# Decay rows by broadcast transfer, a shorter value product, and weight tails doubled by engines in a recurrent mixer with FFT and MLP

## The chip, the cores and the metric

One Trainium2 chip (trn2), one of its cores. The metric is the device time of one execution in microseconds. Three runs of the kernel before gave 452.97 to 453.72, median 453.53. A further execution was recorded by the hardware profiler.

## The reference

Three blocks follow one another on 4 batches, 768 positions, 8 heads of 40 (320 channels):

```python
for t in range(S):                       # 1: gated recurrent attention
    m_new  = np.maximum(f_gate[:, :, t] + m, i_gate[:, :, t])
    f_stab = np.exp(f_gate[:, :, t] + m - m_new)
    i_stab = np.exp(i_gate[:, :, t] - m_new)
    C = f_stab * C + i_stab * einsum(v, k);  n = f_stab * n + i_stab * k
    y[:, :, t] = sigmoid(o_gate) * (C q) / max(|n q|, 1)
gate = sigmoid(causal 5-tap convolution of x)      # 2: gated value
x    = (gate * (x @ w_val)) @ w_out
u  = x + real(fft(fft(x, axis=1), axis=2))          # 3: FFT mixing
un = layernorm(u)
out = u + relu(un @ w_ch1) @ w_ch2                  # 320 -> 1280 -> 320
```

All weights come as float64 bit patterns (two 32-bit words) and are turned into float32 on the chip.

## The kernel before, in words

**How it is written.** The functions in `mixer_kernel` only record instructions in units (`_Plan.add`). `_Plan.emit` (line 288) then issues the units in the order of the table `ORDER`, found beforehand; the table `CELL` gives every tile its slot of SBUF or bank of PSUM, and `FILLS` says where matmuls on a tile of ones stand that compute nothing. Each engine works through its own instructions in order. All instructions issued there have line 305 in the profile, so groups are told apart by tile names. Banks of PSUM are all called `bank`. Transfers are issued by SP, in order too.

**Attention.** It goes in chunks of 128 positions (`c` 0 to 5 for each batch `b`), each made of two halves of 64. `a_fb` puts the decay factors of 64 positions on all partitions (`fb`): in the first four chunks of batch 0 with 16 small float32 matmuls from `f0`, from then on with one 128x512 matmul of a 0/1 table `sel` and the rows `gsp`, which hold a high and a low part of the factors (`prologue_spread` writes both parts to a DRAM scratch `scr`, `gate_rows` loads them for a batch). `a_pre` runs a scan over `fb` on DVE, which gives the decay matrix `d`, and scales values and keys (`kvo`) on POOL. `a_pv` issues, on TensorE, the state product (`cc,e`), the scores of the next chunk (`qk`, in `s_mm`), in batches 1 to 3 the state update (`kvo`, in `u_mm`) and last `kvo,d`, which adds to the same PSUM columns from other rows of the array. Between `cc,e` and `kvo,d` TensorE must have finished: in batches 1 to 3 a `nop` on SP's queue (line 309) waits for the last matmul of the state product and releases the next group; in batch 0 and in the last chunk of each batch a `drain` on TensorE does so. `a_fin` divides by max(|nq|, 1).

**Gated value** (twice a batch, 384 positions each): `p_conv` (four taps of five on DVE, 128x384), `p_val` (for each of three blocks `j` of channels 8 matmuls of 384 columns: high and low parts of weights and of x, for the 64 channels left over the tiles `wvT`, `wvU`), `p_g`, `p_z` (`w_out`).

**FFT, norm, MLP** for each batch: `b_s` (length 768, tables `cs`, a correction row `ex` by `exr`, 193 columns), `b_d` (`dmat`), `b_ln`, `b_ut`, then for three row blocks `m_1` (16 matmuls of 256 columns, tiles `w1..`) and `m_2` (12 of 320, `w2..`), five times each; `hh` and `hl` are high and low part of the hidden layer.

**Weights.** `w_main` and `w_tails` load raw words (`raw`), `to_f32` turns them into float32 (`mk`: one operation on ACT, one on POOL or DVE, three on DVE), and ACT and POOL split them into high and low part. `w_tails` handles the last 64 rows of `w_val`, `w_out` and `w1`; it makes `th` and `tl` and doubles them onto both halves of the partitions by 24 transfers from SBUF to SBUF.

## Time and profile before

| what | value |
|---|---|
| median of 3 runs | 453.53 us |
| the profiled execution: its time / its span | 455.05 us / 453.1 us |
| busy: TensorE matmul, DVE, ACT, POOL | 435.7, 327.0, 175.0, 158.5 us |
| granted TensorE clock, mean | 0.996 |
| DMA moved | 39.83 MB |

The span runs from the first to the last instruction, and 1.95 us lie around it in this execution. PE is TensorE's matmul, PEld its weight load, SPq the transfers that SP issues. A float32 matmul stands as two records, one of float32r as one. Durations of matmuls are modelled and overlap; how far apart two starts lie tells what one takes of the engine.

### The profile page before, as it was taken

To read this page: it belongs to the slowest core of one execution; us is meant where nothing else is said; L and a number is where in the kernel's file an instruction comes from. 1 tells how busy PE (TensorE), PEld (TensorE's weight loads), DVE (VectorE), ACT (ScalarE), POOL (GpSimd) and SP (SyncE) were. 2 spreads that over 40 slices of the span, in tenths; PEclk is the share of its full clock that TensorE was granted. 3 is DMA by queue.
4 is the path that set the end of the run, shared out by engine and by line. 5 is a ranking of instruction groups with operands and counts; after the bars stand their busy time and mean duration, and the time that the engine had idled before them with its cause. 6 is when DMAs were issued, how large, how long until landed. Compare 5 with 4: busy or idle time off the path is not lost.

```text
span 453.1 us, 13800 instructions
## 1 busy us (share of the span) xinstructions
PE 435.7 (96%) x5758; PEld 411.4 (91%) x5758; DVE 327.0 (72%) x810; ACT 175.0 (39%) x412; POOL 158.5 (35%) x210
## 2 busy tenths in 40 slices
PE   9988898889999999999999999999999999999996
PEld 8876778689999999998999999989999999999996
DVE  7999799989989876787487965768856745743221
ACT  4337555455254533134333533325335322333110
POOL 4666136486573333154322333436022120100000
PEclk9999899999999999999999999999999999999999
DMA  6669767931542700013205200323000000000101
GB/s 205 194 190 253 227 191 244 250 115 41 163 128 57 206 1 2 1 39 82 89 17 159 98 1 23 132 63 112 14 18 17 1 30 0 1 30 1 43 16 58
DMA packets 23300, 39.83 MB, mean 88 GB/s; under 512 B 4752, under 2 KB 14288, under 8 KB 23240
## 3 DMA queue, kind: packets, MB, share of 16 engines
q1 hardware_dynamic: 23192, 38.90, 29.0%
q8 instruction: 45, 0.74, 0.7%
q14 instruction: 15, 0.12, 0.1%
q0 software_dynamic: 48, 0.07, 0.1%
HBM read 32.77 MB, written 4.23 MB: 82 GB/s over the span
## 4 chain that ended last, share of the span: by engine, by line
PE 75%; DVE 15%; issue 3%; ACT 2%; POOL 2%; DMA 2%; SPq 0%; DVEq 0%; ACTq 0%; POOLq 0%
PE bank L305 74%; DVE mk L305 5%; DVE d L305 2%; DVE z L305 1%; DMA qk<-in_qk_dram 1%; POOL kvo L305 1%; DVE bank L305 1%; PE bank L368 1%; PE bank L361 1%; DVE bs L305 1%; DVE uu L305 1%; DVE hl L305 1%; DMA woU<-tl 1%; DVE gg L305 1%; DVE cc L305 1%
## 5 line engine op out<-in xcount | busy, mean ns | idle before, releaser
L305 PE MATMUL bank<-uu,w1H 128*128 128x256 f32 x480 | 93.4, 287 | 1.7 <-issue 0.9
L305 PEld LDWEIGHTS bank<-uu,w1H 128*128 128x128 f32 x480 | 74.8, 190 | 3.4 <-issue 1.1
L305 PE MATMUL bank<-w2H,hh 128*128 128x320 f32 x240 | 75.4, 322 | 0.0
L305 PE MATMUL bank<-w2L,hh 128*128 128x320 f32 x240 | 72.2, 309 | 0.0
L305 PE MATMUL bank<-uu,w1L 128*128 128x256 f32 x240 | 67.7, 282 | 0.0
L305 ACT ACTIVATE hh<-bank 128x512 fp32r<-128x512 f32 x60 | 35.1, 597 | 66.3 <-PE bank L305 63.4
L305 DVE SCALAR_TENSOR_TENSOR hl<-bank,hh 128x512 fp32r<-128x512 f32 x60 | 40.4, 684 | 20.1 <-ACT hh L305 14.7
L305 PE MATMUL bank<-w2H,hl 128*128 128x320 f32 x240 | 54.6, 309 | 0.0
L305 DVE SCALAR_TENSOR_TENSOR bank<-xT,cw,bank 128x384 f32<-128x384 f32 x84 | 50.2, 616 | 2.7 <-ACT bank L305 1.9
L305 PEld LDWEIGHTS bank<-w2H,hh 128*128 128x128 f32 x240 | 45.1, 188 | 0.8 <-issue 0.3
L305 PEld LDWEIGHTS bank<-uu,w1L 128*128 128x128 f32 x240 | 45.5, 189 | 0.0
L305 PEld LDWEIGHTS bank<-w2L,hh 128*128 128x128 f32 x240 | 45.2, 189 | 0.1
L305 POOL TENSOR_TENSOR cc<-cc,fcol 128x164 f32<-128x164 f32 x40 | 18.9, 473 | 71.6 <-DVE cc L305 49.6
L305 DVE TENSOR_TENSOR z<-z,bank 128x161 f32<-128x161 f32 (+2 forms) x76 | 27.1, 374 | 20.0 <-PE bank L305 18.4
L305 PEld LDWEIGHTS bank<-w2H,hl 128*128 128x128 f32 x240 | 40.1, 188 | 0.0
L305 PE MATMUL bank<-uu,w1U 128*128 128x256 f32 x120 | 33.9, 282 | 0.0
L305 POOL TENSOR_TENSOR gL<-gg,gH 128x384 fp32r<-128x384 f32 x16 | 17.4, 1092 | 46.7 <-ACT gH L305 41.7
L305 PE MATMUL bank<-uu,w1T 128*128 128x256 f32 x120 | 33.6, 280 | 0.0
L305 DVE TENSOR_TENSOR_SCAN d<-bank,pat 128x512 f32<-128x512 f32 x24 | 29.0, 1211 | 4.9 <-PE bank L305 4.6
L305 POOL TENSOR_TENSOR kvo<-kvo,r 128x320 f32<-128x320 f32 x24 | 17.4, 723 | 35.7 <-DVE r L305 32.1
L305 POOL TENSOR_TENSOR e<-e,qk 128x512 f32<-128x512 f32 (+1 forms) x18 | 21.9, 1214 | 9.0 <-DMA qk<-in_qk_dram 3.7
L305 ACT ACTIVATE r<-bank 128x8 f32<-128x8 f32 x24 | 4.3, 178 | 50.9 <-PE bank L305 43.8
(153 smaller groups left out, 1016.7 us busy)
## 6 DMA issues: line engine op xcount, KB each, us to landing
kvo<-in_kvo_dram SPq DMA_DIRECT2D x24, 484.0 KB
qk<-in_qk_dram SPq DMA_DIRECT2D x48, 160.0 KB
raw<-in_w_dram SPq DMA_DIRECT2D x9, 640.0 KB
out_dram<-z SPq DMA_DIRECT2D x24, 160.0 KB
e<-sce SPq DMA_DIRECT2D x30, 80.0 KB
cs<-in_c_cs_dram SPq DMA_DIRECT2D x2, 386.0 KB
raw<-in_w_val_dram SPq DMA_DIRECT2D x1, 640.0 KB
raw<-in_w_dram SPq DMA_DIRECT2D x4, 160.0 KB
```

What stands on the lines that cost most here:

```text
L305: i = getattr(engine, method)(*a, **k)
L361: nc.tensor.matmul(out=banks()[:, k, 0:L], lhsT=a, rhs=a, start=True, stop=True)
L368: nc.tensor.matmul(out=banks()[:, n % 6, m:m + L], lhsT=a, rhs=a, start=True, stop=True)
```

## The change

1. **Decay rows.** `scr` holds the plain float32 factors, once. From batch 1 on `a_fb` loads the rows of each half chunk straight into the tile `d` by a transfer that repeats them on 64 partitions (36 transfers in all), and the scan works in place. `sel`, `gsp` and `gate_rows` are gone. All six chunks of batch 0 use the small matmuls (`FB0` 6 instead of 4).
2. **Value product.** For block `j` 2 `p_val` issues 5 matmuls instead of 8: the first 64 columns of the weight block hold low parts, the other 64 the high parts, so one pass gives both products on two halves of the partitions. `p_conv` writes the gate of that block twice (64 partitions each), `p_g` makes a copy `gC` on ACT, and `p_z` uses it with `woU`, whose upper half then holds high parts.
3. **Weight tails.** Engines write both halves: 16 copies of 64x320 on ACT and 6 subtractions of 64x320 on POOL replace three copies and three subtractions of 128x320 and the 24 transfers.
4. **Order on TensorE.** All drains in `a_pv` are now `nop`s on SP's queue with keys (24 in all instead of 15), and the units are cut there, so that `ORDER` can put other work between.
5. **Tables.** The zero halves of `cs` and `dmat` and all of `exr` are set by POOL and not loaded; the correction product has 96 columns instead of 193.
6. **Small ones.** DVE's copies and memsets of 12 columns of `xT` go to ACT; |nq| stays in PSUM; in batch 0 the small tiles of `b_ln` lie in PSUM.
7. `ORDER`, `CELL` and `FILLS` are new throughout: 66 fill matmuls instead of 45.

```diff
-FB0 = 4
+FB0 = 6
+LNP = (0,)
 ORDER = [
...
-                if k.pop("drain", False):
-                    engine.drain()
-                before, after = k.pop("before", False), k.pop("after", False)
+                before, after = k.pop("before", 0), k.pop("after", 0)
                 i = getattr(engine, method)(*a, **k)
                 if after:
-                    self.after(i, last)
+                    self.after(i, done[after])
                 if before:
-                    last = self.nop()
-                    self.after(last, i)
+                    done[before] = self.nop()
+                    self.after(done[before], i)
...
+        for t in (wvU, w1U):
+            G.memset(f(t[0:64]), 0.0)
...
-        A.activation(th, m, AF.Copy)
-        less(tl, m, th, 1)
-        for t, ws in ((th, his), (tl, los)):
-            for n in range(2):
-                for o in range(2):
-                    SP.dma_start(out=f(ws[n][64 * o:64 * o + 64]), in_=f(t[64 * n:64 * n + 64, 0]))
+            x = m[64 * n:64 * n + 64, 0]
+            for o in (n, 1 - n):
+                A.activation(his[n][64 * o:64 * o + 64], x, AF.Copy)
+            if cross and n:
+                A.activation(los[n][0:64], x, AF.Copy)
+            l = los[n][64:128] if n else wt("tl", [128, DM], "Z", F32R)[0:64]
+            G.tensor_tensor(l, x, f(his[n][64 * n:64 * n + 64]), op=ALU.subtract)
+            if n == 0:
+                A.activation(los[n][64:128], f(l), AF.Copy)
...
         else:
-            g = gsps[b % 2].rearrange("r (h t) -> r h t", h=H)
-            T.matmul(out=fb, lhsT=sel[:, L * c:L * c + L], rhs=g, start=True, stop=True)
+            fb = wt("d", [128, H, LS], "B")
+            for x in range(2):
+                SP.dma_start(out=fb[64 * x:64 * x + 64],
+                             in_=scr[2 * c + x, b * H:b * H + H, :].unsqueeze(0).to_broadcast([LS, H, LS]))
...
-        d = wt("d", [128, H, LS], "B")
+        d = wt("d", [128, H, LS], "B") if fb.t.banks else fb
...
-            s_mm(b, c + 1, pr, first)
-        order = {"after": True} if merge else {"drain": True}
+            s_mm(b, c + 1, pr, first, key)
+        if not merge:
+            plan.rank += 1
...
-                    go(t["d"][r, h], t["vp"][r, h], x, s, p, True, **(order if p + x + s == 0 else {}))
+                    go(t["d"][r, h], t["vp"][r, h], x, s, p, True,
+                       **({"after": key} if (p, x, s) == (0, 1, 0) else {}))
...
-            ops += [(wvH[:, i, m], xH[:, i]), (wvL[:, i, m], xH[:, i]), (wvH[:, i, m], xL[:, i])]
-        ops += [(wvT[:, m], xH[:, 2]), (wvU[:, m], xH[:, 2])]
+            ops += [(wvH[:, i, m], xH[:, i]), (wvH[:, i, m], xL[:, i])]
+            if j < 2:
+                ops += [(wvL[:, i, m], xH[:, i])]
+        ops += [(wvT[:, m], xH[:, 2])]
+        if j < 2:
+            ops += [(wvU[:, m], xH[:, 2])]
...
-                ops.append((0, ex[:, m], exr))
+                ops.insert(1, (0, ex[:, m], exr, NQ - Q // 2))
```

Three places in the new order. **TensorE, the last of the six value blocks of batch 0** (`xH`, `xL` are x's parts, `wvH` to `wvU` the weights'). Before:

```order
L305 MATMUL bank<-xH,wvH 128x384
L305 MATMUL bank<-xH,wvL 128x384
L305 MATMUL bank<-xL,wvH 128x384
L305 MATMUL bank<-xH,wvH 128x384
L305 MATMUL bank<-xH,wvL 128x384
L305 MATMUL bank<-xL,wvH 128x384
L305 MATMUL bank<-xH,wvT 128x384
L305 MATMUL bank<-xH,wvU 128x384
L305 MATMUL bank<-woH,gH 128x320
```

and of the change:

```order
L305 MATMUL bank<-xH,wvH 128x384
L305 MATMUL bank<-xL,wvH 128x384
L305 MATMUL bank<-xH,wvH 128x384
L305 MATMUL bank<-xL,wvH 128x384
L305 MATMUL bank<-xH,wvT 128x384
L305 MATMUL bank<-woH,gH 128x320
```

Three matmuls are gone from this block, as from the third block of every half batch.

**DVE, where the last weights are turned into float32** (`mk`; `hl` is the MLP's low part, `d<-bank,d` the decay matrix times the scores). Before:

```order
L305 SCALAR_TENSOR_TENSOR mk<-raw,mk 128x640
L305 MEMSET xT 128x3x4
L305 BN_STATS bs<-z 128x6
L305 TENSOR_TENSOR cc_318<-cc_318,bank 128x164
L305 SCALAR_TENSOR_TENSOR mk<-raw,mk 128x640
L305 SCALAR_TENSOR_TENSOR hl<-bank,hh 128x512
L305 TENSOR_TENSOR d<-bank,d 128x2x4x64
```

and of the change:

```order
L305 SCALAR_TENSOR_TENSOR mk<-raw,mk 128x640
L305 SCALAR_TENSOR_TENSOR hl<-bank,hh 128x512
L305 TENSOR_TENSOR x<-bank,kvo 128x2x4x40
L305 SCALAR_TENSOR_TENSOR hl<-bank,hh 128x512
L305 TENSOR_TENSOR cc_414<-cc_414,bank 128x164
L305 BN_STATS bs<-z 128x6
L305 TENSOR_TENSOR d<-bank,d 128x2x4x64
```

Before, the last `mk` stands ahead of the sixth `hl` of the program; now ahead of the fifth.

**SP, around the tables of the FFT in batch 0.** Before (`wvU<-tl` and the like are tails doubled by transfer):

```order
L305 DMA raw<-in_w_dram 64x640
L305 DMA wvU<-tl 64x320
L305 DMA raw<-in_w_dram 128x2x640
L305 DMA w1T<-th 64x320
L305 DMA raw<-in_w_dram 128x2x640
L305 DMA sce<-eg 32x768
L305 DMA woU<-tl 64x320
```

and of the change:

```order
L305 DMA raw<-in_w_dram 128x2x640
L305 DMA sce<-eg 32x768
L305 DMA raw<-in_w_dram 128x2x640
L305 DMA cs<-in_c_cs_dram 128x2x386
L305 DMA d<-scr 64x512
L305 DMA cs<-in_c_cs_dram 64x2x193
L305 DMA d<-scr 64x512
L305 DMA raw<-in_w_dram 128x2x640
```

The tails' transfers are gone, and broadcast rows stand between loads of raw weights. This listing leaves `nop`s out: those of the last two chunks of batch 0 stand right behind `cs` 128x2x386, so behind the two `raw` loads ahead of it.

## Rows read from the trace of the kernel before

**Rows 1.** The page: busy time, and the span in 40 slices.
```profile
PE 435.7 (96%) x5758; PEld 411.4 (91%) x5758; DVE 327.0 (72%) x810; ACT 175.0 (39%) x412; POOL 158.5 (35%) x210
PE   9988898889999999999999999999999999999996
DVE  7999799989989876787487965768856745743221
PEclk9999899999999999999999999999999999999999
```
**Rows 2.** Busy time of each engine in five stretches (engines, clock, DMA share, GB/s).
```profile
0.00:45.00 45.00, 40.26 (x889) 35.07 (x893) 40.13 (x86) 21.87 (x55) 26.63 (x41) 1.00 0.74 210
45.00:95.80 50.80, 44.13 (x442) 37.56 (x435) 46.06 (x110) 28.28 (x68) 23.25 (x26) 0.97 0.77 227
95.80:122.40 26.60, 26.36 (x523) 25.31 (x523) 25.84 (x58) 9.61 (x22) 17.96 (x20) 1.00 0.24 76
122.40:449.70 327.30, 324.98 (x3916) 313.50 (x3916) 214.54 (x559) 115.23 (x271) 90.66 (x126) 1.00 0.17 51
449.70:453.10 3.40, 0.00 (x0) 0.00 (x0) 0.46 (x1) 0.00 (x0) 0.00 (x0) 1.00 0.15 53
```
**Rows 3.** The chain that ended last: start, us, what; early pieces, then the longest.
```profile
32.20 2.52 DMA woU<-tl
34.72 0.97 ACT dg L305 x3
...
49.30 1.15 DVE mk L305 x2
...
62.94 1.86 DVE mk L305 x3
...
121.80 0.61 DVE hl L305
122.46 26.36 PE bank L305 x422
...
299.15 39.84 PE bank L305 x645
339.10 110.55 PE bank L305 x842
449.68 0.49 DVE z L305
```
**Rows 4.** TensorE's matmul groups from 122.4 us on: busy us, mean ns.
```profile
L305 PE MATMUL bank<-xH,wvL 128*128 128x384 f32 x36 | 12.1, 337 | 0.0
L305 PE MATMUL bank<-xH,wvU 128*128 128x384 f32 x18 | 6.1, 337 | 0.0
L305 PE MATMUL bank<-gsp,sel 128*128 128x512 f32 x14 | 5.8, 427 | 0.0
L305 PE MATMUL bank<-exr,ex 128*128 128x193 f32 x6 | 1.5, 326 | 0.0
L305 PE MATMUL bank<-exr,ex 128*64 128x193 f32 x6 | 1.5, 326 | 0.0
```
**Rows 5.** TensorE in order of time, part of a value product (start, us).
```profile
350.33 0.34 PE L305 MATMUL bank<-xH,wvH 128*128 128x384 f32 x1
350.50 0.33 PE L305 MATMUL bank<-xH,wvL 128*128 128x384 f32 x1
350.67 0.34 PE L305 MATMUL bank<-xL,wvH 128*128 128x384 f32 x1
```
**Rows 6.** TensorE in order of time around a drain, the last chunk of batch 3.
```profile
338.32 0.68 PE L305 MATMUL bank<-cc,e 40*64 40x41 f32 x32
339.10 0.68 PE L305 MATMUL bank<-kvo,d 64*64 64x41 f32 x32
339.71 0.41 PE L305 MATMUL bank<-w2H,hh 128*128 128x320 f32 x1
```
**Rows 7.** DVE, then POOL, in order of time early in the program.
```profile
7.47 1.57 DVE L305 TENSOR_TENSOR fs<-gf,mx 32x512 f32<-32x512 f32 x1
9.08 0.68 DVE L305 TENSOR_TENSOR fs<-fs,mx 32x512 f32<-32x512 f32 x1
...
7.31 1.19 POOL L305 TENSOR_TENSOR gi<-gi,mx 32x512 f32<-32x512 f32 x1 [2.63 <-DVE mx L305]
```
**Rows 8.** What SP's queue waited for up to 130 us (us in total, times, longest).
```profile
SPq L309 <- PE bank L305: 17.9, 3, 8.3
SPq L305 <- DVE mk L305: 10.0, 3, 5.0
SPq L305 <- DMA raw<-in_w_dram: 2.7, 2, 2.3
```
**Rows 9.** The page: transfers; then one issue on SP's queue.
```profile
q1 hardware_dynamic: 23192, 38.90, 29.0%
87.22 0.39 SPq L305 DMA_DIRECT2D e<-sce  x1
```

**Rows 10.** ACT and POOL up to 122.4 us: groups, busy us, mean ns.
```profile
L305 ACT ACTIVATE gH<-gg 128x384 fp32r<-128x384 f32 x6 | 3.1, 519 | 4.8 <-DVE gg L305 4.8
L305 ACT ACTIVATE th<-mk 128x320 fp32r<-128x320 f32 x3 | 1.4, 468 | 0.0
L305 POOL TENSOR_TENSOR tl<-mk,th 128x320 fp32r<-128x320 f32 x3 | 2.8, 940 | 0.1
L305 POOL TENSOR_TENSOR fl<-f,fh 32x768 fp32r<-32x768 f32 x1 | 1.8, 1812 | 0.0
```

**Rows 11.** The page: DVE's scans, busy us, mean ns.
```profile
L305 DVE TENSOR_TENSOR_SCAN d<-bank,pat 128x512 f32<-128x512 f32 x24 | 29.0, 1211 | 4.9 <-PE bank L305 4.6
```

More of the change, by code (lines that the diff above doesn't have):

```diff
@@ L290, in emit @@
         self.warm()
-        last = None
+        done = {}
         held = [t for t in self.tiles if t.kind is not None]
@@ L327, in mixer_kernel @@
     c_ep: bass.AP,
-    c_sel: bass.AP,
     c_cs: bass.AP,
     c_d: bass.AP,
-    c_ex: bass.AP,
     out: bass.AP,
@@ L383, in mixer_kernel @@
     epat = epatp[0:32]
-    sel = ct("sel", [128, S], F32R)
-    gsps = [ct("gsp%d" % n, [128, H * LS], F32R) for n in range(2)]
-    cs = [ct("cs%d" % t, [128, 4, NQ]) for t in range(2)]
+    cs = ct("cs", [128, 2, 4, NQ])
     dmat = ct("dmat", [128, 2, 2, NL])
-    exr = ct("exr", [128, NQ])
+    exr = ct("exr", [128, Q // 2])
     ex = ct("ex", [128, 192])
@@ L393, in mixer_kernel @@
     wvH = ct("wvH", [128, 2, 384], F32R)
-    wvL = ct("wvL", [128, 2, 384], F32R)
+    wvL = ct("wvL", [128, 2, 320], F32R)
     wvT = ct("wvT", [128, 384], F32R)
-    wvU = ct("wvU", [128, 384], F32R)
+    wvU = ct("wvU", [128, 320], F32R)
     woH = ct("woH", [128, 2, DM], F32R)
@@ L430, in prologue_pads @@
             G.memset(t, 0.0)
-        for t, n in ((gsps[0], 4), (sel, 6), (gsps[1], 4)):
-            A.activation(t.rearrange("p (a n) -> p a n", n=L), ones.unsqueeze(1).to_broadcast([128, n, L]), AF.Copy,
-                         scale=0.0)
-    def gate_rows(b):
-        SP.dma_start(out=f(gsps[b % 2][0:24]),
-                     in_=scr[:, :, b * H:b * H + H].rearrange("n g h t -> (n g) (h t)"))
+        for t in (wvU, w1U):
+            G.memset(f(t[0:64]), 0.0)
     def prologue_gates():
@@ L443, in prologue_gates @@
         SP.dma_start(out=gi, in_=ig)
-        SP.dma_start(out=pat, in_=c_pat)
+        SP.dma_start(out=ident, in_=c_pat)
+        for x in (slice(0, LS), slice(LS, L)):
+            A.activation(ipat[x].rearrange("p (h t) -> p h t", t=LS),
+                         ident[x, x].unsqueeze(1).to_broadcast([LS, H, LS]), AF.Copy)
         SP.dma_start(out=epat, in_=c_ep)
@@ L574, in weights_vo @@
     def weights_vo():
-        w_main(w_val[0:256, :], wvH[:, :, 0:320], wvL[:, :, 0:320], (wvH[:, :, 320:384], wvL[:, :, 320:384]))
-        w_tails((w_val[256:320, :], w_out[256:320, :]), (wvT[:, 0:320], woT), (wvU[:, 0:320], woU),
-                ((wvT[:, 320:384], wvU[:, 320:384]), None))
+        w_main(w_val[0:256, :], wvH[:, :, 0:320], wvL, wvH[:, :, 320:384])
+        w_tails((w_val[256:320, :], w_out[256:320, :]), (wvT[:, 0:320], woT), (wvU, woU), wvT[:, 320:384], True)
         w_main(w_out[0:256, :], woH, woL)
@@ L659, in pair, with s_mm @@
         return t
-    def s_mm(b, c, t, first):
+    def s_mm(b, c, t, first, key=0):
         sp = t[:, :, 0:4 * LS].rearrange("p s (a n) -> p s a n", a=4)
@@ L669, in s_mm @@
                     T.matmul(out=sp[64 * x:64 * x + 64, s, p, :], lhsT=k[r, p, m], rhs=q[r, p, m],
-                             start=(x, s) not in first, stop=True, skip_group_check=True)
+                             start=(x, s) not in first, stop=True, skip_group_check=True,
+                             **({"before": key} if key and p + x + s == 5 else {}))
                     first.add((x, s))
@@ L728, in a_pv @@
         first = set()
-        merge = b in MERGE and c + 1 < NC
+        merge, key = b in MERGE and c + 1 < NC, 1 + b * NC + c
         def go(lhsT, rhs, x, s, p, last, **m):
@@ L744, in a_pv @@
                     go(t["e"][r, p, LS * x:LS * x + LS], t["cc"][x][r, p], x, s, p, False,
-                       **({"before": True} if merge and p + x + s == 5 else {}))
+                       **({"before": key} if p + x + s == 5 and (merge or c + 1 == NC) else {}))
         if merge:
@@ L1096, in mixer_kernel @@
                     run("spread", prologue_spread)
-                if n == 0:
-                    run("rows", gate_rows, b)
                 run("fb", a_fb, b, n)
@@ L1151, in _constants @@
     c = {}
-    c["c_pat"] = np.concatenate([np.eye(128), np.tile(np.eye(64), (2, 8))], 1).astype(np.float32)
+    c["c_pat"] = np.eye(128).astype(np.float32)
     h, m = np.arange(32)[:, None], np.arange(128)[None, :]
```

104 lines of the change are left out of this document (54 added, 50 removed), and 261 rows, old and new, of tables (CELL, ORDER).

## The prediction

> **What bounds the kernel now.** I read the page first: TensorE is busy for 435.7 us of a span of 453.1, DVE for 327.0 [rows 1]. An average over stages says little, so the next view is the stretches [rows 2] beside the slices of the page [rows 1]. Until 95.8 us TensorE has gaps (40.3 of 45.0 and 44.1 of 50.8 us) and DVE is the fuller engine (40.1 and 46.1): here the weights are decoded. From 95.8 to 122.4 us both are full (26.4 and 25.8 of 26.6). From 122.4 to 449.7 us TensorE is busy for 325.0 of 327.3 us and DVE for two thirds. The chain says the same [rows 3]: many short pieces of DVE (`mk`, `hl`) until 122.4 us, then long runs of TensorE, the last one 110.55 us long. The granted clock is at its full level, 2.4 GHz, all through the late stretch. So the program is a DVE stage of about 122 us, a TensorE stage of 327 us, and 3.4 us of last transfer. A matmul removed from the late stage shortens the span by what it takes of TensorE; one removed early only makes a gap that is there already longer.
>
> **The change, part by part.** *Value product.* Eight blocks lose three matmuls each; six of these blocks lie in batches 1 to 3, and from 122.4 us on the trace has all 36 + 18 = 54 matmuls with `wvL` and `wvU`, of which a third, 18, go [rows 4]. Their mean of 337 ns overlaps with the neighbours; starts lie 0.17 us apart (350.33, 350.50, 350.67) [rows 5]. 18 x 0.173 = **3.1 us**. The extra copy `gC` on ACT is like `gH`, 0.52 us [rows 10], eight times; ACT is busy for a third of the late stage [rows 2], and TensorE has the MLP of the batch before to do meanwhile. I cost it at nothing; without that cover it would be up to 0.5 us for each half batch, six times, 3 us.
>
> *Decay rows.* 14 matmuls with `sel` lie after 122.4 us [rows 4]. At the value product's rate, 0.173 us for 384 columns, 512 columns take 0.23 us; 14 x 0.23 = **3.2 us**. The rows now come by 36 transfers. Each issue costs SP some 0.39 us, as one of `e<-sce` does [rows 9], together 14 us over more than 300 us of a queue that is otherwise little used there. Each transfer is 64 x 8 pieces of 256 bytes, 18,432 pieces in all. Taken at the mean of all packets there are now, 29% of 16 engines over 453.1 us for 23,192 packets, 91 ns [rows 9], they would fill the 16 engines for 105 us in all, spread over more than 300 us, beside a DMA share of 17% [rows 2]. So bandwidth is no bound even at that price, and pieces this small should take less. The Trainium skill's page "DMA: Bandwidth & Descriptors" (Specifications) speaks against the change here: below 512 bytes a transfer leaves line rate. Doubling the price above would still leave the transfers hidden, by my estimate; no run so far shows it.
>
> *Correction row.* 12 records of 193 columns become 96 columns [rows 4]. By the same rate for two passes in each record, 97 columns fewer are 0.08 us: **1.0 us**.
>
> *Drains.* In batch 3 the state product starts at 338.32, runs 0.68, and `kvo,d` starts at 339.10, 0.10 us after its end; groups that need no drain overlap, as `w2H` at 339.71 starts 0.07 us before the end of `kvo,d` [rows 6]. With other units put in the gap about 0.25 us each is won, three times in the late stage: **0.8 us**. The six drains of batch 0 lie in the DVE stage: nothing, at best 6 x 0.25 = 1.5 us.
>
> *Early stage.* The 21 further fills stand in batch 0, where TensorE waits: nothing. Its two `sel` chunks cost small matmuls now: nothing, for the same reason. The six shortened matmuls there: nothing. ACT gets 16 tail copies, at most 0.47 us each, 7.5 us, and loses 1.4 of `th`; POOL gets six subtractions for three, at most 5.6 us for 2.8, and loses 1.8 of `fl` [rows 10]. ACT is half busy there, POOL too [rows 2]. The 24 transfers that go take one wait off the chain, 2.52 us before `woU<-tl` landed [rows 3], but DVE has other work around it. Where the order puts the last `mk` ahead of the fifth `hl` instead of the sixth, that is one operation's difference. DVE's own work up to there stays about the same: small copies and memsets leave, nothing large. So I leave the start of the TensorE stage at 122.4 us, with bounds of 5 us earlier (the wait for `woU`, the drains, 1 us of small work) and 4.5 us later (the scans, below).
>
> The sum is 3.1 + 3.2 + 1.0 + 0.8 = 8.1 us, all in the TensorE stage. The profiled execution took 455.05 us, so it would take 447.0. It stood 1.5 us above the median of 453.53; against the median the forecast is **445.4 us**.
>
> **The rivals.** *The scans collide with POOL.* The scan read PSUM and one SBUF tile; from batch 1 on it reads two SBUF tiles. The trace shows what two such inputs can cost: an operation on two tiles of 32x512 in SBUF took 1.57 us while POOL ran one of its own from 7.31 to 8.50, and the next of the same shape 0.68 alone [rows 7]. That is 0.89 us for a collision. The Trainium skill has the rule: the page "SBUF — State Buffer" (Who interferes with whom) says that a DVE instruction with two SBUF inputs contends with a GpSimd instruction that reads SBUF, and that one waits for the whole of the other. The trace agrees with it in that row. In the late stage DVE has a third of its time free, so 13 of the 18 scans cost nothing. About five are due before the TensorE stage begins, where DVE and POOL are both busy: 5 x 0.89 = 4.5 us given back, 449.9 us. For it: POOL is busy for 18.0 of 26.6 us between 95.8 and 122.4 [rows 2]. Against it: all five would have to meet one of POOL's operations near its start. Chance 0.13.
>
> *SP's queue holds the `nop`s of batch 0* (the slower side). A drain waits for TensorE alone. A `nop` waits its turn behind transfers whose slots are not free: SP waited 10.0 us in three waits for `mk` to free raw words, the longest 5.0, and 2.7 us for a load to land [rows 8]. Two `nop`s of batch 0 stand behind `raw` loads. While one is held, `kvo,d` is, then `a_fin` on DVE, and behind that in DVE's order the decoding of weights: this stage has no slack. If all 12.7 us fell on `nop`s, the time would be 445.4 + 12.7 = 458.1 us; it turns slower beyond 8.1 us of such holds. For it: in batch 1 to 3 the same `nop`s work, but SP is idle there, waiting for TensorE (17.9 us in three [rows 8]), so those rows say nothing about a crowded queue. Against it: 24 transfers leave just this part of the queue. Chance 0.09.
>
> *The early stage gets shorter as well.* The wait for the tails (2.5), the drains (1.5) and 1 us of small DVE work all count: 5 us less, 440.4 us. For it: each of them has a row or a count. Against it: in a full stage one wait's end mostly uncovers the next. Chance 0.13.
>
> *The freed time turns into waits.* DVE, ACT or a late `d` transfer does not follow the faster TensorE, and the 8.1 us stay as gaps: 453.5 us. Against it: only 2.3 us of 327.3 are not busy now [rows 2], and DVE a third free. Chance 0.04.
>
> **How the numbers follow.** Forecast 445.4 us, chance 0.61. What a measurement can tell from no change is about 0.2%, 0.9 us. Faster: 0.61 + 0.13 + 0.13 = 0.87; same 0.04; slower 0.09. The range reaches from the shorter early stage (440.4, 440 rounded) to somewhat beyond the collision of scans (449.9) with the uncovered `gC` copies in part, 451. It leaves out the 0.13 of the second and fourth rival, and little more.
>
> **What would show it.** Right: the last long runs of TensorE start near 122 us and end near 441.5; the groups `xH,wvL` and `xH,wvU` have 24 and 12 matmuls in the late stage, no `gsp,sel`; TensorE's waits there stay below 4 us. Collision: scans `d<-d` with a mean well above the 1.21 us that they take now [rows 11], and a later start of the long runs. Held `nop`s: TensorE waiting for SP in the first 60 us. The forecast is wrong if the DVE stage ends more than 4 us away from 122.4, or if TensorE shows new gaps behind `d<-scr`.

## The result and the profile after

The changed kernel took a median of 456.15 us (454.71 to 458.52, 10 runs) beside 453.31 us (450.90 to 453.72, 10 runs) of the kernel before: 1.0074 times, 95% interval 1.0051 to 1.0097. It is slower by 2.8 us where the forecast had 445.4 us and a range up to 451. The profiled execution took 456.57 us, near its median; that of before took 455.05, 1.7 above the 453.31. Below, medians are over all executions of a kernel, and ratios leave out the slow ones, over 1.5% above the fastest of their kernel (one of h1_value_row and of h3_drains, two of s1_start and of b4_splits).

The page of the changed kernel, for [rows 1] (DVE is VectorE, ACT ScalarE, POOL GpSimd, SP SyncE):

```profile
PE 434.4 (96%) x5820; PEld 410.5 (90%) x5820; DVE 333.7 (73%) x801; ACT 189.6 (42%) x448; POOL 170.2 (37%) x218
PE   9987999878999999999999999999999999999996
DVE  6699899899999887699785785776876756643220
PEclk9999899989999999999999999999999999999999
```

The page hardly differs: TensorE 1.3 us less, DVE 6.7 and POOL 11.7 us more. The stretches of [rows 2] say more. The changed kernel, with one more stretch that ends at its first MLP matmul:

```profile
0.00:45.00 45.00, 38.56 (x858) 35.46 (x859) 37.26 (x75) 20.54 (x51) 23.07 (x36) 1.00 0.64 188
45.00:95.80 50.80, 45.09 (x447) 35.86 (x447) 46.25 (x93) 31.76 (x75) 30.95 (x35) 0.95 0.72 203
95.80:122.40 26.60, 24.13 (x332) 22.57 (x330) 24.85 (x64) 13.54 (x30) 19.32 (x19) 0.97 0.27 81
122.40:449.70 327.30, 325.91 (x4184) 316.09 (x4184) 224.83 (x571) 123.75 (x293) 96.81 (x129) 1.00 0.21 63
...
0.00:105.90 105.90, 91.67 (x1414) 78.15 (x1414) 92.91 (x192) 58.18 (x139) 60.51 (x77) 0.97 0.64 181
```

and the kernel before up to its own first MLP matmul:

```profile
0.00:95.80 95.80, 84.39 (x1319) 72.63 (x1320) 86.19 (x195) 50.15 (x121) 49.88 (x66) 0.98 0.76 219
```

A stretch that is equal by the clock is not equal by the work. So I cut both programs at the same piece of work, the first MLP matmul. Before it is

```profile
95.81 0.48 PE L305 MATMUL bank<-uu,w1H 128*128 128x256 f32 x2 [0.61 <-DVE uu L305]
```

and in the changed kernel

```profile
105.94 0.47 PE L305 MATMUL bank<-uu,w1H 128*128 128x256 f32 x2 [1.85 <-DVE uu L305]
```

**The late part gained, the early part lost.** From this matmul to the end of the span it was 453.1 - 95.8 = 357.3 us and is 454.7 - 105.9 = 348.8: 8.5 us less, where the forecast had 8.1. Up to it the program takes 10.1 us more. (Together that is 1.6 us; the medians differ by 2.8, as the profiled execution of before is a long one.) DVE is busy for 92.9 instead of 86.2 us there and idle for 13.0 instead of 9.6: 6.7 + 3.4 = 10.1. DVE's busier time is hardly more work. In every profiled execution I priced every instruction of DVE up to this matmul at its bare duration (of its operation and shape over all these traces, the duration that a tenth of them undercut): 89.4 us before, 90.6 now. Over these prices they ran 8.1 us before and 13.7 now. Below I call that the slowed time. (Busy time counts overlapping instructions once and so is below the sum of the two.)

Which instructions are slowed shows in DVE's groups up to the first MLP matmul (busy us, mean ns). Before:

```profile
L305 DVE SCALAR_TENSOR_TENSOR mk<-raw,mk 128x640 int32<-128x640 int32 x16 | 14.9, 937 | 0.0
L305 DVE TENSOR_SCALAR mk<-mk 128x640 int32<-128x640 int32 x8 | 4.7, 604 | 0.0
L305 DVE TENSOR_SCALAR mk<-mk 128x640 f32<-128x640 f32 x8 | 4.4, 550 | 0.0
```

Now:

```profile
L305 DVE SCALAR_TENSOR_TENSOR mk<-raw,mk 128x640 int32<-128x640 int32 x16 | 15.1, 951 | 0.0
L305 DVE TENSOR_SCALAR mk<-mk 128x640 f32<-128x640 f32 x9 | 6.9, 771 | 0.0
L305 DVE TENSOR_SCALAR mk<-mk 128x640 int32<-128x640 int32 x9 | 6.6, 733 | 0.0
...
L305 DVE TENSOR_TENSOR_SCAN d<-d,ipat 128x512 f32<-128x512 f32 x2 | 3.8, 1892 | 0.0
L305 DVE TENSOR_SCALAR mk<-mk 128x320 f32<-128x320 f32 x3 | 2.2, 734 | 0.0
L305 DVE TENSOR_SCALAR mk<-mk 128x320 int32<-128x320 int32 x3 | 0.9, 310 | 0.0
```

It is the weight decoding with one input, `mk<-mk`: the mean of its f32 form of 640 columns rose from 0.55 to 0.77 us. The instruction itself did not change. DVE in order of time, from a stretch of the changed kernel:

```profile
79.71 1.79 DVE L305 TENSOR_SCALAR mk<-mk 128x640 f32<-128x640 f32 x1
...
82.61 0.48 DVE L305 TENSOR_SCALAR mk<-mk 128x640 f32<-128x640 f32 x1
...
85.79 0.47 DVE L305 TENSOR_SCALAR mk<-mk 128x640 int32<-128x640 int32 x1
...
87.25 1.82 DVE L305 TENSOR_SCALAR mk<-mk 128x640 int32<-128x640 int32 x1
...
101.73 2.57 DVE L305 TENSOR_TENSOR_SCAN d<-d,ipat 128x512 f32<-128x512 f32 x1
```

and POOL at the same time:

```profile
79.50 1.64 POOL L305 TENSOR_TENSOR w2L<-mk,w2H 128x640 fp32r<-128x640 f32 x1 [2.12 <-ACT w2H L305]
...
85.72 0.93 POOL L305 TENSOR_TENSOR eo<-es 128x159 f32<-128x159 f32 x1 [0.33 <-DVE es L305]
86.61 2.12 POOL L305 TENSOR_TENSOR w1L<-mk,w1H 128x640 fp32r<-128x640 f32 x1
...
101.42 1.80 POOL L305 TENSOR_TENSOR w2L<-mk,w2H 128x640 fp32r<-128x640 f32 x1
```

The 0.47 us of the one are 1.79 us where POOL's difference of another weight began 0.21 us earlier, and 1.82 where the next began 0.64 us earlier. The Trainium skill's page "SBUF — State Buffer" (Who interferes with whom) has this: besides instructions with two SBUF inputs, those of one input that can use both ports (it names `tensor_scalar`) contend with GpSimd, and the one that comes second waits for the whole of the other. These rows agree: 79.71 + 1.79 = 81.50 lies 0.36 us behind the end of POOL's instruction at 81.14, and 87.25 + 1.82 = 89.07 lies 0.34 us behind its end at 88.73. It is not always DVE that is late: at 85.79 the decoding took its 0.47 us, though POOL's `eo<-es` ran at the same time by the profile. Laid over each other, `mk<-mk` and `mk<-raw,mk` ran beside POOL for 22.0 us up to the first MLP matmul; before it was 11.5.

The late stage has the counts that [rows 4] promised:

```profile
L305 PE MATMUL bank<-xH,wvL 128*128 128x384 f32 x24 | 8.1, 338 | 0.0
L305 PE MATMUL bank<-xH,wvU 128*128 128x384 f32 x12 | 4.0, 337 | 0.0
L305 PE MATMUL bank<-exr,ex 128*128 128x96 f32 x6 | 1.1, 261 | 0.0
L305 PE MATMUL bank<-exr,ex 128*64 128x96 f32 x6 | 1.0, 246 | 0.0
```

There is no `gsp,sel`, and TensorE's last run in the chain of waits, for [rows 3], is

```profile
234.74 215.71 PE bank L305 x2466
```

**The granted clock differs too.** Ahead of its first MLP matmul, TensorE's clock stood at its lower level, 1.2 GHz, twice in this execution of the changed kernel, and once before, from 51.8 us. The two stretches of the changed kernel (PE, PEld, DVE, ACT, POOL, clock, DMA share, GB/s):

```profile
46.10:49.50 3.40, 3.40 (x21) 2.74 (x15) 3.30 (x8) 2.14 (x7) 1.86 (x4) 0.50 0.68 186
93.90:97.30 3.40, 3.40 (x12) 2.24 (x12) 3.30 (x8) 0.56 (x2) 0.70 (x1) 0.50 0.89 288
```

Its ten executions had a mean clock of 0.986 to 0.996; of 101 executions of the kernel before, beside the experiments below, 94 had 0.995 to 1.000. Two of the changed kernel at 0.996 took 454.71 and 455.16 us, where 33 of the kernel before have a median of 453.38; two at 0.992 took 456.26 and 456.57, where five of before have 455.33. So at the same clock some 1 to 1.5 us of the 2.8 seem to be left, from few executions. Whether TensorE's waits lower the clock here, or the clock lengthens the waits, no run tells.

### The profile page after: what moved, and what is told of

It is laid out like the page before. It is cut to its first block, busy times and chain, and to the rows that moved or that the text cites. A ratio compares the mean times of both kernels' runs of the same rounds, so it can differ in the third digit from the quotient of the medians.

```text
span 454.7 us, 13940 instructions
## 1 busy us (share of the span) xinstructions
PE 434.4 (96%) x5820; PEld 410.5 (90%) x5820; DVE 333.7 (73%) x801; ACT 189.6 (42%) x448; POOL 170.2 (37%) x218
## 2 busy tenths in 40 slices
DMA packets 23971, 41.57 MB, mean 91 GB/s; under 512 B 4452, under 2 KB 13284, under 8 KB 23908
## 4 chain that ended last, share of the span: by engine, by line
PE 67%; DVE 7%; issue 1%; POOL 1%; DMA 1%; ACT 0%; DVEq 0%; ACTq 0%
PE bank L305 67%; DVE d L305 2%; DVE bank L305 1%; DVE mk L305 1%; DMA d<-scr 1%; DVE z L305 1%; DVE hl L305 1%; POOL kvo L305 0%; POOL w2L L305 0%; POOL w1L L305 0%; DVE cc L305 0%; DVE xL L305 0%; DVE uu L305 0%; ACT gate L305 0%; DVE r L305 0%
## 5 line engine op out<-in xcount | busy, mean ns | idle before, releaser
L305 PE MATMUL bank<-uu,w1H 128*128 128x256 f32 x480 | 91.7, 283 | 2.3 <-DVE uu L305 1.9
L305 POOL TENSOR_TENSOR cc<-cc,fcol 128x164 f32<-128x164 f32 x40 | 22.1, 553 | 73.6 <-DVE cc L305 56.7
L305 DVE TENSOR_TENSOR z<-z,bank 128x320 f32<-128x320 f32 (+2 forms) x76 | 26.6, 373 | 22.7 <-PE bank L305 22.2
L305 POOL TENSOR_TENSOR kvo<-kvo,r 128x320 f32<-128x320 f32 x24 | 18.7, 780 | 22.6 <-DVE r L305 22.5
L305 POOL TENSOR_TENSOR e<-e,qk 128x512 f32<-128x512 f32 (+1 forms) x18 | 23.2, 1296 | 10.2 <-DMA d<-scr 7.7
L305 ACT ACTIVATE gate<-bank 128x384 f32<-128x384 f32 (+1 forms) x32 | 15.6, 488 | 25.2 <-DVE bank L305 20.6
L305 ACT ACTIVATE bank<-bank 128x8 f32<-128x8 f32 (+1 forms) x32 | 6.0, 187 | 48.2 <-DVE d L305 37.5
```

The costliest lines, as they stand in the source:

```text
L305: i = getattr(engine, method)(*a, **k)
```

## The experiments

All runs, each beside the kernel before on the same chip. "First MLP" is the start of the first MLP matmul in the profiled execution, "busy / idle" is DVE up to it, "slowed" as above, "rest" the span from there to its end. All of these are of one execution, and they vary: five kernels with the changed kernel's TensorE work behind that matmul (after, s1_start, a2_drain, a3_memset, a4_splits) have rests of 348.0 to 349.3 us, two with that of the kernel before (before, b4_splits) 357.3 and 355.9.

| run | us, median | ratio to before, 95% interval | first MLP | busy / idle | slowed | rest |
|---|---|---|---|---|---|---|
| before | 453.31 | | 95.8 | 86.2 / 9.6 | 8.1 | 357.3 |
| after | 456.15 | 1.0074 (1.0051 to 1.0097) | 105.9 | 92.9 / 13.0 | 13.7 | 348.8 |
| h1_value_row | 452.85 | 0.9989 (0.9972 to 1.0006) | 95.6 | 87.5 / 8.1 | 9.7 | 354.7 |
| h1b_gate | 451.30 | 0.9956 (0.9927 to 0.9986) | 94.0 | 86.5 / 7.5 | 8.4 | 354.7 |
| h1c | 452.31 | 0.9974 (0.9953 to 0.9995) | 97.7 | 87.5 / 10.2 | 9.4 | 354.6 |
| a11_eight | 457.66 | 1.0103 (1.0067 to 1.0139) | 103.9 | 90.3 / 13.6 | 10.9 | 351.8 |
| a4_splits | 451.19 | 0.9952 (0.9931 to 0.9973) | 100.3 | 87.4 / 12.9 | 7.9 | 348.0 |
| b4_splits | 455.81 | 1.0037 (1.0010 to 1.0065) | 97.7 | 84.4 / 13.3 | 5.9 | 355.9 |
| a9_tensor | 468.81 | 1.0323 (1.0288 to 1.0358) | 116.2 | 87.8 / 28.4 | 7.9 | 351.2 |
| a10_both | 462.33 | 1.0193 (1.0167 to 1.0220) | 111.6 | 87.5 / 24.1 | 7.6 | 348.2 |
| a12_four | 455.10 | 1.0022 (0.9991 to 1.0054) | 103.6 | 88.0 / 15.6 | 8.5 | 349.9 |
| s1_start | 455.80 | 1.0033 (1.0004 to 1.0063) | 104.7 | 92.4 / 12.3 | 13.1 | 349.3 |
| a2_drain | 456.54 | 1.0053 (1.0026 to 1.0080) | 105.6 | 91.6 / 14.0 | 12.0 | 348.3 |
| a3_memset | 457.89 | 1.0087 (1.0055 to 1.0120) | 106.7 | 91.0 / 15.8 | 11.5 | 348.1 |
| h2_decay_rows | 467.55 | 1.0303 (1.0259 to 1.0348) | 102.4 | 84.8 / 17.6 | 6.3 | 362.3 |
| h2b_rows | 470.04 | 1.0348 (1.0306 to 1.0391) | 100.3 | 85.4 / 14.9 | 6.9 | 368.2 |
| h3_drains | 466.63 | 1.0273 (1.0228 to 1.0318) | 100.2 | 85.2 / 15.1 | 6.6 | 363.1 |
| o4_order | 529.45 | 1.1676 (1.1626 to 1.1725) | 150.5 | 92.6 / 57.9 | 12.6 | 376.7 |

### The terms of the late stage

**h1_value_row**: the kernel before in its own order, with the shorter value product (the gate in two halves, `gC` beside `gH`) and the 96 columns.

```diff
+            if j < 2:
+                ops += [(wvL[:, i, m], xH[:, i])]
...
-                ops.append((0, ex[:, m], exr))
+                ops.insert(1, (0, ex[:, m], exr[:, k0:NQ], k0))
```

> The kernel before, in its own order of work, with two parts of the change alone: the third block of the value product in five passes of TensorE instead of eight (24 matmuls of 384 columns fewer), and the correction row as 96 columns instead of 193. Nothing else of the early stage moves. Theory 1 (the late TensorE stage gives what was forecast, and it is the early stage of the changed kernel, in its new order, that loses it again): 3.1 + 1.0 us less, about 449.2 us, with the first MLP matmul where it was, near 96 us. Rival (matmuls left out of the late stage come back as waits of TensorE, so the forecast sum was never there): within 1 us of 453.3.

The rest is 2.6 us shorter than in the kernel before, two thirds of 4.1, with the early part as long as there. The medians lie 0.7 us apart (453.56 for the kernel before in these runs), and the interval holds 1: the time is the rival's, the shorter rest speaks in part for the theory. What TensorE waits for between 122 and 440 us is new:

```profile
PE bank L307 <- ACT gate L307: 2.6, 4, 1.0
```

**h1b_gate** takes the second gate instruction away; the lower half then holds another block's gate.

```diff
-            A.activation(g[64:128], a[64:128], AF.Sigmoid)
...
-            A.activation(g[0:64], a[64:128], AF.Sigmoid)
...
+            A.activation(g, a, AF.Sigmoid)
```

> The kernel before with five value passes and the short correction row, as in h1_value_row, but with the third block's gate in one instruction of ScalarE instead of two halves (the lower half then holds another gate, so that the low part of the third block's product is a different value). In the trace of h1_value_row TensorE waits 2.6 us in the late stage, four times, for a gate; the kernel before has no such wait. Theory (the forecast saving is there, but the second half instruction of the gate, costed at nothing, gives 2 us of it back as a wait): 1 to 2 us less than h1_value_row, 450.5 to 451.5 us, and no waits for gates. Rival (the waits only move to another instruction): within 0.5 us of h1_value_row's 452.6.

The median is 1.55 us lower, as the theory had it, but the rest is 354.7 us in both: by the trace the waits only moved,

```profile
PE bank L307 <- DVE x L307: 1.0, 1, 1.0
PE bank L307 <- ACT gate L307: 0.9, 2, 0.5
```

and the rival holds for the late stage. In these two executions the gain lies ahead of the first MLP matmul; the next run shows how little two executions tell there. With the second half of the gate left out, this kernel is faster than the kernel before, at most 0.9986 times its time.

**h1c** adds the `nop` for the last chunk of batches 1 to 3.

```diff
-        order = {"after": True} if merge else {"drain": True}
+        order = {"after": True} if b in MERGE else {"drain": True}
```

> The kernel before with five value passes, one gate instruction, the short correction row (h1b_gate), and the wait for an empty TensorE ahead of the last chunk of batches 1 to 3 replaced by a no-operation of SyncE. Theory 1: the three late drains are worth 0.5 to 0.9 us: 450.4 to 450.8 us. Rival (SyncE's queue holds TensorE as long as the drain did): within 0.4 us of h1b_gate's 451.3.

The rest is 354.6 instead of 354.7: in the old order, where nothing else stands in the gap, a drain is worth nothing. The rival holds for the rest; the median is 1.0 us above h1b_gate's, which neither theory had. Both kernels issue the same instructions ahead of their first MLP matmul, yet it starts at 94.0 in the one execution and 97.7 in the other. So the early part of single executions differs by 3.7 us, and only medians compare it.

**a11_eight** undoes the value product's term in the changed kernel, with other weight columns in the three passes.

```diff
-            if j < 2:
-                ops += [(wvL[:, i, m], xH[:, i])]
+            ml_ = m if j < 2 else slice(192, 320)
+            ops += [(wvL[:, i, ml_], xH[:, i])]
...
+        ops += [(wvU[:, ml_], xH[:, 2])]
```

> The changed kernel with the three value passes of the third block put back (with other columns of the low weights, so that this block's value differs; the count and size of the matmuls are those of the kernel before). This undoes one term of the forecast where the late stage is the changed kernel's own. Theory 1 (the term was right, and only the early stage took it away): 18 matmuls of 0.17 us after the first MLP matmul, 2.5 to 3.6 us more than the changed kernel, 458.7 to 459.8 us. Rival (TensorE's late stage has gaps into which they fall, and the term was never there): less than 1 us more.

The late groups have [rows 4]'s counts again:

```profile
L305 PE MATMUL bank<-xH,wvL 128*128 128x384 f32 x36 | 12.1, 337 | 0.0
L305 PE MATMUL bank<-xH,wvU 128*128 128x384 f32 x18 | 6.1, 338 | 0.0
```

and the rest is 3.0 us longer: within the 1.3 us by which rests vary, the forecast's 3.1 holds. The median rose by 1.5 us only, between what theory and rival had; why, no run shows. In the profiled execution the early part was 2.1 us shorter, which may be chance.

### Small parts of the early loss

**s1_start**: six entries of the table `ORDER` moved within the first 15 us, and the first fill.

```diff
-    (26, 25, 0), (86, 3, 6),
+    (26, 8, 0), (86, 3, 6),
```

> The changed kernel with its first 15 us in the order of the kernel before: VectorE's subtraction for the input gates right behind the first maximum scan, its exponential first on ScalarE, the pattern of the scans built after the first decays, and 8 instead of 25 filling matmuls ahead of the first transposes. All else as in the changed kernel. Theory 1, part a (the start costs about 3 us, seen in the first chunk's output at 29.4 instead of 26.4 us, and VectorE bounds the stage from there on): 2 to 3 us less than the changed kernel, 453 to 454 us, first chunk's output near 27 us. Rival (what is lost at the start is hidden by later waits): within 0.5 us of the changed kernel's 456.1.

The first chunk's output came at 29.1 us, not at 27, the first MLP matmul 1.2 us earlier. The medians differ by 0.35 us, the ratios' intervals overlap: the rival's number. But the clock hides something here. Seven of the twelve executions had a mean granted clock of 0.984 to 0.987; the other five, at 0.991 to 0.995, took 452.24 to 455.51, median 453.71, while the six of the changed kernel at 0.991 to 0.996 have 456.15. In the profiled execution, with 17 fills fewer, TensorE stood at 1.2 GHz from 11.1 to 14.5 us, where the changed kernel's stood at 2.4. So the new start may cost the 2 us or so that the theory had, and the fills may earn them back by the clock; executions picked by their clock do not show it.

**a2_drain**: `nop`s of batch 0 back to drains.

```diff
-                       **({"after": key} if (p, x, s) == (0, 1, 0) else {}))
+                       **({"after" if b else "drain": key} if (p, x, s) == ((0, 1, 0) if b else (0, 0, 0)) else {}))
```

> The changed kernel, with the wait of batch 0's attention for SyncE's no-operation put back to a wait for an empty TensorE, as the kernel before has it there. Theory 1, part c (in batch 0 the no-operations stand behind transfers in SyncE's queue, some 1 us in all at 44 to 46 us): 0.5 to 1.5 us less than the changed kernel, 454.5 to 455.5 us. Rival 1 (the holds of the no-operations are hidden by VectorE): within 0.5 us of 456.1. Rival 2 (SyncE is what makes the early stage long): 3 us less or more.

No gain. One such hold stands in the trace of the changed kernel, 0.98 us on TensorE in batch 0,

```profile
45.59 0.68 PE L305 MATMUL bank<-kvo,d 64*64 64x41 f32 x31 [0.98 <-issue]
```

and taking it away moves nothing. Rival 1 holds.

**a3_memset**: zeros from ScalarE.

```diff
-        G.memset(cs[64:128, :, 2], 0.0)
+        A.activation(cs[64:128, :, 2], c0(64, NQ), AF.Copy, scale=0.0)
```

> The changed kernel, with the zeros that it now writes itself (low half of two weight tails, the zero halves of the cosine and sine tables and of the second table) written by ScalarE instead of GpSimd. Theory 1, part b: 1.5 us of VectorE's slowed time stand beside these writes: 1 to 2 us less than the changed kernel, 454 to 455 us. Rival (where the zeros are written makes no difference): within 0.5 us of 456.1.

DVE's slowed time fell by 2.2 us, its idle time rose by 2.8, and the time did not fall (457.89 us, above both theories). Moving POOL's added writes gains nothing.

### DVE beside POOL

**a4_splits**: all differences off POOL.

```diff
-            WLO.tensor_tensor(l, x, f(h), op=ALU.subtract)
+            A.activation(l, x, AF.Copy)
...
-            G.tensor_tensor(l, x, f(his[n][64 * n:64 * n + 64]), op=ALU.subtract)
+            A.activation(l, x, AF.Copy)
```

> The changed kernel, with the low parts of all weights left out of GpSimd: ScalarE writes a plain copy of the weight in place of GpSimd's difference of weight and high part (the low parts then hold another value; every instruction is still issued, on the other engine). In the trace of the changed kernel VectorE does about the same work up to the first MLP matmul as before (90.4 against 89.4 us at bare durations) but its instructions run 13.6 instead of 8.0 us over these, above all the weight decoding beside GpSimd's differences, and it stands idle 13.0 instead of 9.6 us. Theory 1, part b (VectorE and GpSimd slow each other, and the new order puts decoding beside differences): 5 to 7 us of the slowed time go, the first MLP matmul comes at 100 to 102 instead of 105.9 us, time 450 to 452 us. Rival (the attention's chain of waits sets the pace in the new order and VectorE only waits longer when it is faster): first MLP matmul within 2 us of 105.9, time 455 or more.

456.15 became 451.19 us. DVE's groups up to the first MLP matmul:

```profile
L305 DVE TENSOR_SCALAR mk<-mk 128x640 int32<-128x640 int32 x9 | 4.8, 538 | 0.0
L305 DVE TENSOR_SCALAR mk<-mk 128x640 f32<-128x640 f32 x9 | 4.3, 479 | 0.0
```

The f32 form is back at its bare 0.48 us. Slowed time fell from 13.7 to 7.9 us, idle time stayed (13.0 and 12.9), and the first MLP matmul came 5.7 us earlier: the sum closes. The clock is not the reason: five executions at 0.996 took 449.44 to 451.65 us, two of the changed kernel at 0.996 took 454.71 and 455.16. A second difference of this edit remains: a low part no longer waits for its high part. If that shorter way were what won, DVE should stand idle for less, and it does not.

**b4_splits**: the same in the kernel before, whose tails go through the same function.

```diff
-            WLO.tensor_tensor(l, x, f(h), op=ALU.subtract)
+            A.activation(l, x, AF.Copy)
```

> The same edit on the kernel before: low parts of all weights as plain copies on ScalarE instead of differences on GpSimd. Theory 1, part b: there only some 2 to 3 us of VectorE's slowed time stand beside those differences, so the gain is at most half of that in the changed kernel: 451 to 453 us, first MLP matmul at 93 to 95 us. Rival (the collisions cost both kernels the same, and the new order is slower for another reason): as large a gain as in the changed kernel, 4 us or more.

Slowed time falls by 2.2 us only, as expected, but idle time rises by 3.7, and the kernel gets slower, by 0.1% to 0.65%, which neither theory had. (At a granted clock of 1.000 four executions took 451.33 to 455.85 us, much as before; at 0.996 four took 455.42 to 456.87.) The same edit wins 5.0 us in the one kernel and nothing in the other. So POOL's differences did not hold up the old order; they do hold up the new one.

**a9_tensor, a10_both, a12_four** keep the low parts whole. TensorE makes seven of the eleven large differences in banks that are free until the first MLP sums; a10 adds the start of s1; a12 does so with the four earliest alone.

```diff
+                for i in range(2):
+                    T.matmul(out=ps[:, 6 + i, 160:480], lhsT=ident, rhs=x[:, i], start=True, stop=False)
+                    T.matmul(out=ps[:, 6 + i, 160:480], lhsT=nid, rhs=h[:, i], start=False, stop=True)
+                A.activation(l, ps[:, 6:8, 160:480], AF.Copy)
```

> The changed kernel, computing all that it computes, with seven of the eleven large differences of weight and high part (those due before the first MLP sums need the PSUM banks) made by TensorE into PSUM, identity times weight less identity times high part, and copied out by ScalarE, instead of by GpSimd. This tells whether the gain of a4_splits came from GpSimd's absence beside VectorE or from the shorter ScalarE copies. Theory 1, part b (GpSimd's presence): VectorE's slowed time up to the first MLP matmul 9 to 11 instead of 13.6 us, that matmul at 101 to 104 instead of 105.9 us, time 451.5 to 454.5 us. Rival (the gain came from the shorter way to the low parts, and seven times 1.4 us of TensorE and as many copies in the attention's queues cost more): 456 us or more, first MLP matmul not earlier than 105.

Slowed time went to 7.9 us, as low as with plain copies, so it is the absence of POOL's differences that relieves DVE, whatever takes their place. But idle time rose to 28.4 us and the kernel lost 12.7 us, as the rival had it. DVE's longest waits up to there:

```profile
DVE ve L316 <- ACT w1L L316: 6.3, 1, 6.3
DVE mk L316 <- ACT mk L316: 2.7, 1, 2.7
```

The layer norm stands behind a copy that waits for TensorE.

a10_both, with s1's order and fill besides:

```diff
-    (26, 25, 0), (86, 3, 6),
+    (26, 8, 0), (86, 3, 6),
```

> The last kernel with the start of s1_start as well (input gates first, short first fill), which brought the first MLP matmul 1.2 us forward. Theory 1 (the parts of the early loss add up): 1 us less than a9_tensor. Rival (the start is hidden behind the decoding once the collisions are fewer): within 0.4 us of a9_tensor.

6.5 us less than a9_tensor: far more than the 1 us expected. In the profiled executions 4.6 us lie ahead of the first MLP matmul, nearly all idle time, and 3.0 behind it, where a9_tensor's had TensorE at 1.2 GHz for 3.4 us from 169.1 us. That an early start is worth more where waits, not work, set the pace would explain the first part; it is not shown.

a12_four (the number is a place in `ORDER`):

```diff
-            plan.mute = ORDER.index(n) < 564
+            plan.mute = ORDER.index(n) < 500
```

> As a10_both, but only the four earliest of the large differences on TensorE; the other seven stay with GpSimd. In a9_tensor VectorE's slowed time fell from 13.7 to 7.8 us as theory 1, part b, has it, but its idle time rose from 13.0 to 28.4 us, 6.3 of it in one wait of the layer norm for ScalarE, which stood waiting for TensorE's difference for the first MLP weights. Theory (slowed time and idle time are separate terms, and the idle time came from those three late differences): slowed time 9 to 11 us, idle time 13 to 17 us, first MLP matmul at 102 to 105 us, time 453 to 456 us. Rival (every difference on TensorE holds up the attention): idle time over 20 us, time 459 us or more.

Nearly all as the theory had it: slowed 8.5 (it had 9 to 11), idle 15.6, 103.6 us, 455.10 us. But that is only 1 us less than the changed kernel, with 5.2 us less slowed time: 2.6 of these came back as idle time. It doesn't beat the kernel before (the interval holds 1).

### Decay rows and the order

**h2_decay_rows** adds the broadcast transfers to h1_value_row, into three buffers.

```diff
-            T.matmul(out=fb, lhsT=sel[:, L * c:L * c + L], rhs=g, start=True, stop=True)
+            fb = fbS[SCAN.index(b * NC + c) % 3]
...
+            SP.dma_start(out=fbS[r % 3][64 * x:64 * x + 64],
+                         in_=scr[0, 2 * c + x, b * H:b * H + H, :].unsqueeze(0).to_broadcast([LS, H, LS]))
```

> The last kernel, and besides the decay rows of batches 1 to 3 (and of the last two chunks of batch 0) brought by two broadcast transfers each into three buffers, asked for two chunks ahead, instead of by a matmul and a PSUM bank; the split of the decays in two parts falls away with it. Theory 1: another 3.2 us of TensorE fall away, less at most 1 us for scans that now read two operands from SBUF beside GpSimd: 446 to 447 us. Rival (scans of two SBUF operands collide with GpSimd and hold the chain up): 449 us or more, with scans of over 2 us where they were 1.2.

14.7 us more than h1_value_row. Neither holds: it is far from 446, and the scans take 1.38 us, 0.17 more, not over 2. SP waited for a buffer, among other things:

```profile
SPq L309 <- DVE d L309: 31.7, 3, 19.7
```

TensorE's granted clock was 0.974 in the profiled execution and 1.000 in that of h1_value_row, so part of the loss is TensorE at its lower level.

**h3_drains** adds to this kernel the `nop`s of h1c. Expected were 0.5 to 0.9 us less, three waits fewer, or by the rival no gain. It took 466.63 us against 467.55, in executions from 461.46 to 469.17, and its rest is 0.8 us longer: no gain that can be told from none.

**h2b_rows**: six buffers and, to make room, one `gC` instead of two.

```diff
-    fbS = [ct("fb%d" % n, [128, H, LS]) for n in range(3)]
+    fbS = [ct("fb%d" % n, [128, H, LS]) for n in range(6)]
...
-    gCs = [ct("gC%d" % n, [128, HALF], F32R) for n in range(2)]
+    gCs = [ct("gC%d" % n, [128, HALF], F32R) for n in range(1)]
```

> The kernel before with five value passes, the short correction row and the decay rows by broadcast transfers, as in h2_decay_rows, but with six buffers instead of three, and the first rows of batches 1 and 2 asked for where the kernel before asks for its gate rows. In h2_decay_rows SyncE waited 31.7 us at the decay rows for scans to release a buffer and asked for the next chunk's inputs late; VectorE's scans were only 0.17 us longer each. Theory (decay rows by transfer are cheap for TensorE, but two more issues of about 0.55 us per chunk on SyncE's queue and a wait for a buffer there hold all that stands behind them): with buffers enough 5 us or more of the loss go, 455 to 462 us. Rival (scans of two operands from SBUF are what costs): within 2 us of 467.5.

Those waits went, the time did not (470.04 us). TensorE's longest waits in this run are short ones of many kinds,

```profile
PE bank L309 <- DMA qk<-in_qk_dram: 3.0, 3, 1.2
PE bank L309 <- ACT gate L309: 2.9, 4, 1.2
PE bank L309 <- ACT gC L309: 2.8, 2, 2.0
```

My theory of the buffers falls, and the rival's number is missed too, by 0.5 us; the single `gC` may have cost something of its own. Which of the waits begins the loss stays open; in the changed kernel's order the same kind of transfers come without it.

**o4_order**: the changed kernel's first 560 pieces in the order of the kernel before, by its table alone (`ORDER`, whose rows tell a reader nothing).

> The changed kernel with all its edits, but its first 560 or so pieces of work in the order in which the kernel before has the same pieces, as far as the changed kernel's buffers allow it; pieces that only the changed kernel has stay beside their neighbours; behind these the order is the changed kernel's. Theory 1, part d (the loss lies in the new order, which puts the weight decoding of VectorE in bunches beside GpSimd's differences and ahead of the attention): the first MLP matmul at 97 to 102 us instead of 105.9, VectorE's slowed time down from 13.6 to 8 to 11 us, time 448 to 453 us. Rival (it lies in what the change adds, in whatever order): first MLP matmul at 104 or later, time 455 or more. A third outcome would be a longer time with more waits of VectorE, where the mixture of two orders fits neither.

The third outcome: DVE idle for 57.9 us. It tells nothing on the order's part; that the buffers of the one kernel don't fit the order of the other is likely, but not shown.

## Why the prediction was wrong

**The step that failed** is the early stage: "So I leave the start of the TensorE stage at 122.4 us, with bounds of 5 us earlier [...] and 4.5 us later". By the same piece of work it began 10.1 us later: the first MLP matmul came at 105.9 instead of 95.8 us, and the MLP's 149th, which stood at 122.46, at 132.71. That is twice the bound. The sentence ahead of it, that DVE's own work stays about the same, was right (89.4 and 90.6 us at bare durations). The fault was to take equal work for equal time.

- **The mechanism was in the text, in the wrong place.** The first rival priced a collision of DVE and POOL at 0.89 us from [rows 7], for five scans with two SBUF inputs, 4.5 us at most. Of two such scans ahead of the first MLP matmul one was indeed slowed, to 2.57 us beside `w2L<-mk,w2H`, and it lies on the chain of waits that leads to that matmul; the other took 1.22, and the mean of all 18 is 1.38. But the weight decoding stands in the same stage, with 24 `mk<-mk` before and 26 now. From the page of the Trainium skill I took the rule for two inputs and passed over the one for one input.
- **The order was read for what moved, not for what came to stand beside it.** The listing showed where the last `mk` stands among `hl`. What mattered is which of POOL's differences runs when DVE decodes, on two engines at once: 22.0 us of overlap instead of 11.5. POOL also has more to do there, 60.5 us busy instead of 49.9, so that order and added work both enter; o4_order was to part them and could not.
- **The late stage** held, in part by luck: 8.5 against 8.1 us, in parts that vary by 1.3 us from execution to execution. The value product is right (3.0 against 3.1, a11_eight). The correction row was too large: from starts to the next starts, its 12 late records take 0.87 instead of 1.17 us of TensorE, 0.3 us and not 1.0; 96 columns do not pay in proportion. The decay rows were too small: counted the same way, the 14 late `gsp,sel` held TensorE for 3.8 us, not 3.2. The two errors cancel. The drains' 0.8 is not shown: in the old order they are worth nothing (h1c).
- **The decay transfers** were read wrongly, without effect on the sum: not 18,432 pieces of 256 bytes, but 2,304 packets of 2,048, 64 for each transfer. The page of the profile has 23,971 packets now and had 23,300. So the sentence on pieces below 512 bytes had nothing here to bear on.
- **The SP queue** as a rival had its hold (0.98 us), but a2_drain shows that it costs nothing. That the time came out near this rival's 458.1 us is chance. **The uncovered `gC`**: in the old order the second half of the gate shows as a wait of 2.6 us; taking it away only moved the wait.
- **The fills** were costed at nothing, and s1_start bounds the first of them together with the order of the start: 1.2 us of trace, not resolved in the medians, with a lower clock that may hide up to 2 us.

Of the 10.1 us, 6.7 are busy time of DVE (5.6 slowed and 1.2 bare work, with 0.1 of overlap) and 3.4 idle time. That POOL's weight differences slow DVE is shown three times: slowed time falls to 7.9, 7.9 and 8.5 us in a4_splits, a9_tensor and a12_four. What this costs is known less sharply: a4_splits, where idle time stays, wins 5.0 us; a12_four, where half of it turns into idle time, 1.0. What causes the 3.4 us of idle time no run settles.

## What to carry to other kernels

Cut two traces at the same piece of work, not at the same time, and split the engine that bounds a stage into bare work, slowed work and idle time. Where DVE bounds a stage, look at what POOL does beside each of its instructions, those with one input too. Slowed time that is taken away counts only as far as it doesn't come back as idle time. Compare executions at the same granted clock. A saving on one engine that needs a new order is priced only when the stage that it does not touch is priced in the new order as well.

## What the runs showed that I had not expected

- A decoding instruction of one input takes 0.47 us undelayed and 1.79 to 1.82 where POOL's difference of two inputs began 0.21 to 0.64 us ahead of it; one input is no shelter.
- The same edit, plain copies on ScalarE instead of POOL's differences, won 5.0 us in one order and nothing in another.
- The same early instructions took 94.0 us in one execution and 97.7 in another, with DVE's slowed time 8.4 and 9.4 and its idle time 7.5 and 10.2: how instructions happen to meet adds spread, more of it in waits than in collisions.
